# Strassen's scheme for the last group's product with w4 in an attention and S2-MLP kernel

## The chip, the cores and the metric

The kernel runs on one core of one Trainium2 chip. The metric is the device time of one execution in microseconds (us). Each time is a median over runs of the same kernel.

## The reference, cut to what matters

x has 2048 rows of 512 float32 columns. The two layers below are applied twice, with the same weights:

```python
def _A_ref(x, wqkv, wo):            # 32 heads of 16, window of 8 keys at a stride of 2 rows
    qkv = (x @ wqkv).reshape(B, S, 3, H, Dh)...
    logits = einsum("bhsd,bhswd->bhsw", q, kg) * scale   # kg: keys of rows s, s-2, .. s-14
    attn = softmax(where(mask, logits, -1e9))
    o = einsum("bhsw,bhswd->bhsd", attn, vg)
    return o.reshape(B, S, D) @ wo
def _B_ref(x, w1, w2, w3, w4):      # D = 512, F = 1792
    h = gelu(layernorm(x) @ w1)
    hs = concat(h's four quarters, shifted by +1, -1, +2, -2 rows) @ w2
    x1 = x + hs
    return x1 + gelu(layernorm(x1) @ w3) @ w4
x = x + _A_ref(layernorm(x), wqkv, wo)
x = x + _B_ref(layernorm(x), w1, w2, w3, w4)
```

## The kernel before

**Tiles and groups.** The rows are cut into four blocks of 512 rows, each of four tiles of 128. Two layers of four blocks make eight groups, n = 0 to 7. Because of the row shifts, a group's second half is skewed: `group(n)` (line 1298) gives the tiles (n,1), (n,2), (n-1,3), (n,0), and for group 7 also its own last tile (7,3), so that group 7 has five tiles. A group passes through the normalisation and the product with wqkv (`p1_stream`), attention on VectorE (`p2`), the product with wo and w1 (`p3`, line 1180), the product with w2 with a layernorm and a transpose (`p4`), and the MLP with w3, gelu and w4 (`p5`, line 1491).

**Precision.** An operand of a product is kept as two fp16 parts, high and low. Each block product is three matmuls (`HLS`, line 51: high·high, high·low, low·high), accumulated in PSUM. So the three matmuls of 512 columns that belong to one tile and one chunk of w4 are one product with w4.

**The MLP.** F = 1792 is cut into 14 chunks of 128. For groups 0 to 5 each chunk makes a product with w3, a gelu, a cast into two fp16 parts, and a product with w4 that adds into one PSUM accumulator per tile (`acc`). For groups 6 and 7 (`FAST`, line 1307) the product with w3 goes by Strassen's scheme: `p5_pair` (line 1397) takes two chunks at once, and makes seven products of quarter blocks instead of eight. These use sums of blocks of w3, made once by `sums_w3` (line 993) and kept in DRAM (`w3s_d`), and sums of blocks of x (`sums_x`, line 1310). VectorE and POOL combine the seven products into the two chunks; gelu and the casts follow. The fifth tile of group 7 is computed plainly beside them (`up5`). Then come the products with w4 of the pair, in `p5_pair`'s `down`: for each chunk four tiles by three matmuls of 512 columns, which add into `acc`, and the fifth tile's three.

**Order.** No engine's order is that of the source. Each operation gets a key from the table `PLACES` (line 57), by the order in which it is made; `plan` (line 295) sorts all operations by the key, hands out buffer slots in that order, and the instructions are then issued, on each engine in that order (`InOrder`, line 326). A second table, `OTHER`, says for which operations the second of two engines is taken (`op(key, [(POOL, ...), (DVE, ...)])`). An `after=` argument only restricts the table; on the chip an instruction waits for the data that it reads and for the buffer that it writes. DMAs leave SyncE in order, on eight semaphores in turn: each also waits until the one eight places before it on its semaphore has landed. All instructions are recorded at the helper's line 336 (344 after the change), so groups in the profile are told apart by the names of the tiles, not by lines. The names of tiles that matter: `prod`, `kv`, `q`, `L`, `o` belong to attention; `oT`, `nT` are transposed operands; `g` holds the cast gelu outputs; `w` (and `wq_hl`, slots lent from the weights wqkv after their last use) the streamed weights; `mm` and `acc` are PSUM tiles.

Of the kernel before, what the change touches and what calls it, by code (L numbers as in the profile page):

```python
# [1614 lines left out]
```

## Time and profile before

| | us |
|---|---|
| median of 3 runs (1124.87, 1128.14, 1127.88) | 1127.88 |
| the profiled execution, as it was timed | 1126.82 |
| its span in the profile | 1125.0 |
| busy VectorE (DVE), ScalarE (ACT), GpSimd (POOL) | 936.3, 652.0, 498.4 |
| data moved by DMA, mean rate | 224.00 MB, 199 GB/s |

The page gives, for each engine, the busy time over the span. PE is TensorE's matmuls, PEld its weight loads, which overlap the matmuls. SPq and ACTq stand for the DMAs that SyncE and ScalarE issue. A row of a timeline has the start, the length, the engine, the line, the operation, the output tile, the inputs, the shape and a count xN; in brackets stands the idle time of that engine just before, and what ended it. A windows row has the span of time, its length, then the busy time of PE, PEld, DVE, ACT and POOL with their instruction counts, TensorE's granted clock, the share of DMA engines busy and GB/s. The granted clock is 1.00 in every stretch of this profile.

### The profile page before, as it was taken

What the parts mean: (1) busy time and instruction counts of PE and PEld (TensorE: products, weight loads), DVE (VectorE), ACT (ScalarE), POOL (GpSimd) and SP (SyncE); (2) the same over time, 40 slices, a digit from 0 to 9 for tenths busy, and PEclk for the clock granted to TensorE, in tenths of its full rate; (3) what the DMA queues carried; (4) which work ended last, traced back from release to release, by engine and by line L of the source; (5) the groups of instructions that cost most, each with busy time, mean ns of one, the idle gap of its engine ahead of it and who ended that gap; (6) DMA issues with size and microseconds to landing.
All of it is one profiled execution on the core that took longest, in us unless ns stands there. A gap on an engine that the chain in (4) does not pass through costs nothing.

```text
span 1125.0 us, 16122 instructions
## 1 busy us (share of the span) xinstructions
PE 1106.7 (98%) x5488; PEld 550.7 (49%) x5488; DVE 936.3 (83%) x1065; ACT 652.0 (58%) x1233; POOL 498.4 (44%) x587
## 2 busy tenths in 40 slices
PE   9999999999999999999999999999999999999998
PEld 7544444544444444444444444444444447555764
DVE  5899999999999799788988999778996999746432
ACT  5877785358753576365665566573554654467341
POOL 3569674236722473135544143445623367234230
PEclk9999999999999999999999999999999999999999
DMA  7688999999988589766779868996877769555642
GB/s 215 197 226 225 236 245 262 248 237 239 238 233 241 116 209 193 200 161 167 189 182 222 200 156 221 249 240 174 203 223 198 211 160 243 155 145 111 185 146 61
DMA packets 268994, 224.00 MB, mean 199 GB/s; under 512 B 143688, under 2 KB 205128, under 8 KB 268912
## 3 DMA queue, kind: packets, MB, share of 16 engines
q1 hardware_dynamic: 267296, 221.20, 77.1%
q10 hardware_dynamic: 1616, 1.77, 0.6%
q8 instruction: 43, 0.70, 0.3%
q14 instruction: 39, 0.32, 0.1%
HBM read 143.65 MB, written 41.54 MB: 165 GB/s over the span
## 4 chain that ended last, share of the span: by engine, by line
PE 69%; DVE 14%; POOL 5%; ACT 4%; DMA 3%; issue 3%; SPq 1%; ACTq 0%; DVEq 0%; POOLq 0%
PE mm L336 50%; PE acc L336 19%; DVE prod L336 8%; DVE L L336 2%; POOL small L336 2%; DVE f L336 1%; ACT junk L336 1%; SPq L336 1%; POOL f L336 1%; DMA w<-in_B_w_dram 1%; DVE mx L336 1%; POOL prod L336 1%; ACT f L336 1%; DVE g L336 1%; POOL g L336 1%
## 5 line engine op out<-in xcount | busy, mean ns | idle before, releaser
L336 PE MATMUL acc<-w,g 128*128 128x512 f16 (+1 forms) x1104 | 271.2, 395 | 0.4 <-DVE g L336 0.4
L336 PE MATMUL mm<-wq_hl,xt 128*128 128x512 f16 x1008 | 224.9, 379 | 3.0 <-DMA xt<-f 1.6
L336 PE MATMUL mm<-nT,w 128*128 128x512 f16 (+2 forms) x1110 | 225.3, 355 | 1.8 <-DMA nT<-f 1.4
L336 PEld LDWEIGHTS <-w 128*128 128x128 f16 x1428 | 133.9, 98 | 118.1 <-issue 8.4
L336 PEld LDWEIGHTS <-g 128*128 128x128 f16 x1176 | 114.7, 98 | 135.4 <-DVE g L336 1.4
L336 PEld LDWEIGHTS <-xt 128*128 128x128 f16 x1008 | 98.4, 98 | 121.7 <-issue 3.4
L336 DVE TENSOR_TENSOR prod<-kv,L 128x2048 f32<-128x2048 f32 x64 | 150.4, 2350 | 1.4 <-POOL o L336 0.2
L336 DVE TENSOR_REDUCE L<-prod 128x128 f32<-128x2048 f32 x64 | 146.1, 2283 | 1.1
L336 DVE TENSOR_TENSOR prod<-kv,q 128x2048 f32<-128x2048 f32 x58 | 134.3, 2316 | 5.0 <-DMA q<-q_d 1.9
L336 ACT ACTIVATE mm<-mm,s_w 128x512 f32<-128x512 f32 (+1 forms) x109 | 70.1, 644 | 112.1 <-PE mm L336 111.8
L336 DVE TENSOR_TENSOR prod<-prod 128x1024 f32<-128x1024 f32 (+1 forms) x119 | 124.8, 1049 | 2.5
L336 POOL TENSOR_SCALAR small<-small 128x1 f32<-128x1 f32 (+1 forms) x133 | 65.1, 490 | 103.8 <-ACT junk L336 56.2
L336 POOL TENSOR_TENSOR small<-small,nhalf 128x1 f32<-128x1 f32 (+1 forms) x104 | 90.2, 869 | 46.0 <-ACT small L336 40.6
L336 PE MATMUL mm<-w_hl,h 128*128 128x512 f16 x384 | 86.3, 379 | 0.0
L336 PE MATMUL mm<-nT,w_hl 128*128 128x512 f16 x384 | 85.8, 379 | 0.0
L336 PE MATMUL mm<-wo_hl,oT 128*128 128x512 f16 x336 | 74.2, 379 | 0.0
L336 POOL TENSOR_TENSOR g<-f,g 128x512 f16<-128x512 f32 x34 | 42.5, 1252 | 52.8 <-ACT g L336 26.3
L336 PEld LDWEIGHTS <-oT 128*128 128x128 f16 x426 | 41.7, 98 | 49.3 <-issue 0.6
L336 ACT ACTIVATE ev<-mm,s_kv 128x512 f32<-128x512 f32 x56 | 38.0, 682 | 38.5 <-PE mm L336 31.7
L336 PEld LDWEIGHTS <-w_hl 128*128 128x128 f16 x384 | 37.6, 98 | 44.9
L336 PEld LDWEIGHTS <-h 128*128 128x128 f16 x384 | 37.6, 99 | 44.4 <-POOL h L336 0.2
L336 POOL TENSOR_TENSOR o<-prod 128x256 f32<-128x256 f32 x22 | 16.8, 766 | 89.5 <-DVE prod L336 89.2
(251 smaller groups left out, 1611.1 us busy)
## 6 DMA issues: line engine op xcount, KB each, us to landing
w<-w SPq DMA_DIRECT2D x183, 256.0 KB, 3.7
kv<-kv_d SPq DMA_DIRECT2D x112, 352.0 KB, 5.8
w<-in_B_w_dram SPq DMA_DIRECT2D x56, 256.0 KB, 3.8
kv_d<-ev SPq DMA_DIRECT2D x112, 128.0 KB, 3.5
q_d<-ev SPq DMA_DIRECT2D x28, 256.0 KB, 5.5
w<-g SPq DMA_DIRECT2D x28, 256.0 KB, 3.2
q<-q_d SPq DMA_DIRECT2D x28, 256.0 KB, 4.3
wq_hl<-w SPq DMA_DIRECT2D x27, 256.0 KB, 4.2
```

Of the source, the lines that this page charges most:

```text
L336: i = f(*a, **k).ins
```

## The change

In group 7 the product with w4 for the first four tiles is now made by Strassen's scheme too. It is no longer inside the pairs, but follows after all of them, in seven products over the whole of F ("sweeps"):

- `sums_w4(j)`, for each of the seven pairs: loads two chunks of w4 as float32 (256 KB each), makes two blocks of sums in four operations of 256 columns, casts both into high and low parts, and stores them in DRAM (`w4s_d`, two stores of 256 KB).
- In `p5_pair` of group 7, after the gelu: four operations of 256 columns make the sums `s12`, `s34` of the two chunks' outputs; these two tiles are cast into high and low parts as well. All four casts of a pair are kept until the end, in 28 lent slots of kind `gg`: 16 in the tiles of attention (kv, q, prod, L, o) after group 7's last product with wo, and four each in the weights wo, w1 and w2 after their last use. The products of a pair with w4 are left only for the fifth tile (two times three matmuls of 512 columns).
- `p5_sweep`: seven products, each over seven pairs, each with its own half of a weight block per pair (a DMA of 128 KB in pieces of 512 bytes), for two tile positions q: 14 accumulations of 21 matmuls of 256 columns. Results leave PSUM by 256 columns, and are added to the output rows in place by VectorE (`into_x`).
- The tables `PLACES` and `OTHER` are new as a whole.

The diff, cut to its core (the two tables are left out):

```diff
+    small_w = {n: const.tile([P, 2 * NC * D], F16, name=f"{n}_hl") for n in ("wo", "w1", "w2")}
+    late = ([as16("kv", j, k) for j in range(3) for k in range(2)] + [as16("q", j, 0) for j in range(2)] +
+            [as16("prod", 0, k) for k in range(4)] + [as16("L", j, 0) for j in range(2)] + [as16("o", j, 0) for j in range(2)] +
+            [of_w(n, k) for n in ("wo", "w1", "w2") for k in range(4)])
+        "gg": places("gg", 0, [P, 2 * D], F16, const, late),
+    def sums_w4(j, after):
+        raw = [Buf("w") for _ in range(2)]
+        for m, t in enumerate(raw):
+            dma(0, lambda t=t: f32v(t.t, D), lambda i=2 * j + m: w4_d[P * i:P * (i + 1), :], [], [t], 1.0, after)
+        def sums(e):
+            e.tensor_sub(t12.t[:, h1], b1[:, h2], b1[:, h1])
+            e.tensor_sub(t12.t[:, h2], b2[:, h2], t12.t[:, h1])
+            e.tensor_sub(t34.t[:, h1], b2[:, h2], b1[:, h2])
+            e.tensor_sub(t34.t[:, h2], b2[:, h1], t12.t[:, h2])
+        op(0, [(POOL, 2.5, lambda: sums(G), None), (DVE, 1.5, lambda: sums(V), "lock")], raw, [t12, t34])
+        for m, t in enumerate((t12, t34)):
+            hi_of(0, D, out, src, w, [t, iv4], [hl])
+            rest(0, lambda out=out: out(1), src, w, lambda out=out: out(0), D, [hl, iv4], [t, (hl, 1)])
+            dma(0, lambda m=m: w4s_d[j][:, m], lambda hl=hl: halves(hl.t), [(hl, [0, 1])], [(w4s, (j, m))], 1.0)
...
+        end_group = K > NT
-        gs = [Buf("g") for _ in cs]
+        gs = [Buf("gg" if end_group else "g") for _ in cs]
...
+            def sums(e):
+                a1, a2 = got[0].t, got[1].t
+                e.tensor_add(s12.t[:, L], a1[:, R], a2[:, R])
+                e.tensor_sub(s12.t[:, R], s12.t[:, L], a1[:, L])
+                e.tensor_sub(s34.t[:, L], a1[:, L], a1[:, R])
+                e.tensor_sub(s34.t[:, R], a2[:, L], s12.t[:, R])
...
-            pe(key, 0.6478 * NT, lambda down=down: down(range(NT)), [w, (gs[q], [0, 1])], acc[:NT])
             if gx:
                 pe(key, 0.6478, lambda down=down: down([NT]), [w, (gx, [0, 1])], acc[NT:])
+            else:
+                pe(key, 0.6478 * NT, lambda down=down: down(range(NT)), [w, (gs[q], [0, 1])], acc[:NT])
+    def p5_sweep(n, key, xt_):
+        def product(k):
+            ws = [Buf("w") for _ in range((NP + 1) // 2)]
+            for j in range(NP):
+                dma(key, lambda j=j: hb(ws[j // 2], j % 2), lambda j=j: src(j), [cell(j)], [(ws[j // 2], j % 2)], 0.5, past[-2])
+            for q, kind in enumerate(("mm", "acc")):
+                def sweep(ps=ps, q=q, k=k):
+                    for j in range(NP):
+                        v = halves(kept[j][gi].t)[:, :, 2 * P * gh + P * q:2 * P * gh + P * (q + 1)]
+                        for a, b in HLS:
+                            T.matmul(ps.t[:, L], v[:, a], hb(ws[j // 2], j % 2)[:, b], start=(m == 0), stop=(m == 3 * NP - 1))
+        def into_x(r, h, q, v, rd):
+            dve(key, 0.42, lambda: V.scalar_tensor_tensor(x.t[:, h], v(), s_w4.t, x.t[:, h], ALU.mult, ALU.add), ...)
+        for q, ps in enumerate(product(1)):
+            act(key, 0.42, lambda ps=ps, q=q: A.activation(half(a, q), ps.t[:, L], AF.Copy), [ps], [(a, q)])
+            into_x(0, L, q, lambda q=q: half(a, q), [(a, q)])
...
+        for k, r, h in ((2, 0, L), (3, 0, R), (4, 1, L)):
+            for q, ps in enumerate(product(k)):
+                into_x(r, h, q, lambda ps=ps: ps.t[:, L], [ps])
...
-        acc = [Buf("acc" if k < NT else "mm") for k in range(K)]
+        acc = [Buf("acc" if k < NT or n >= FAST else "mm") for k in range(K)]
...
+        if n == N - 2:
+            for j in range(NP):
+                sums_w4(j, [w2_last[n - 1]])
```

What the new tables make of the order is shown at three places, in rows of the programs as they are issued. A row has the line, the operation, the output tile, its inputs, the shape, and in brackets the semaphores that it waits for (DMAHW0 to DMAHW7 are the eight of the DMAs).

On SyncE, the last loads of weights before the change. They are whole blocks (128x1024) of w3, w4 and the sums of w3, among output rows:

```order
L336 DMA w_193<-w_9_128 128x1024 [waits DMAHW2_49,PE_49]
...
L336 DMA w_170<-w_8_127 128x1024 [waits DMAHW7_49,PE_49]
L336 DMA wq_hl<-w_10_129 128x1024 [waits DMAHW0_49,PE_49]
L336 DMA w_194<-w_11_130 128x1024 [waits DMAHW1_49,PE_49]
L336 DMA w_167<-w_13_132 128x1024 [waits DMAHW2_49,PE_49]
L336 DMA out_dram<-x_200 64x512 [waits DMAHW3_49]
L336 DMA wq_hl<-w3s_139 128x1024 [waits DMAHW4_49,PE_49]
```

On SyncE, the loads after the change of product 2 of the sweeps: seven halves (128x2x256) of the chunks 1, 3, ... 13 of w4, into four slots. The loads of five products are issued ahead of these, and those of product 4 behind them.

```order
L344 DMA w_175<-w_3_125 128x2x256 [waits DMAHW4_49,PE_49]
L344 DMA w_180<-w_5_127 128x2x256 [waits DMAHW5_49,PE_49]
L344 DMA w_201<-w_11_133 128x2x256 [waits DMAHW6_49,PE_49]
L344 DMA w_180<-w_7_129 128x2x256 [waits DMAHW0_49]
L344 DMA w_201<-w_9_131 128x2x256 [waits DMAHW1_49]
L344 DMA wq_hl<-w_13_135 128x2x256 [waits DMAHW2_49,PE_49]
L344 DMA w_175<-w_1_123 128x2x256 [waits DMAHW3_49]
```

The last loads before the change are spread among other transfers, with a wait of their own for PE each; after it seven halves stand in a train, and the last of the train is the one for the first pair.

On TensorE, the last products before the change are the fifth tile's accumulations, with no wait among them:

```order
L336 MATMUL mm_69<-w_194,oT_219 128x512
L336 LDWEIGHTS oT_224
L336 MATMUL mm_69<-wq_hl,oT_224 128x512
L336 LDWEIGHTS oT_224
...
L336 LDWEIGHTS oT_224
L336 MATMUL mm_69<-w_167,oT_224 128x512
```

On TensorE, after the change, near the end of the program: the last matmuls of a sweep of product 3 (into acc_230) and the first of product 2 (into acc_228; `kv_185` and `kv_214` are lent slots, that hold cast gelu outputs here):

```order
L344 MATMUL acc_230<-w_203,w_hl 128x256 [waits DMAHW7_49]
...
L344 LDWEIGHTS kv_185 [waits DMAHW3_49]
L344 MATMUL acc_228<-w_175,kv_185 128x256 [waits DVE_49]
...
L344 MATMUL acc_228<-w_175,kv_214 128x256 [waits DMAHW4_49]
...
L344 MATMUL acc_228<-w_180,prod_208 128x256 [waits DMAHW5_49]
```

In place of 512 columns under no wait there are 256 columns, and a sweep's first weight load now waits for the DMA on semaphore 3, which is the last row of the train above.

On VectorE, in the middle of group 7's attention before the change (`prod` from `kv` and the weights `L`, folded by halves; `h` and `f` belong to group 6's products with w1 and w2):

```order
L336 TENSOR_TENSOR prod_196<-kv_209,L_197 128x2048 [waits DVE_49]
L336 TENSOR_TENSOR prod_196<-prod_196 128x2x512 [waits DVE_49]
L336 SCALAR_TENSOR_TENSOR h_187<-mm_71,c_h,h_187 128x512 [waits Activation_49]
L336 SCALAR_TENSOR_TENSOR h_187<-mm_69,c_h,h_187 128x512 [waits Activation_49]
L336 SCALAR_TENSOR_TENSOR h_187<-mm_73,c_h,h_187 128x512 [waits Activation_49]
L336 TENSOR_TENSOR prod_196<-prod_196 128x2x256 [waits DVE_49]
```

The same place after the change (`w` slots hold raw chunks of w4; `f` and `prod_213` here take the sums of `sums_w4`):

```order
L344 TENSOR_TENSOR f_183<-w_201,f_217 128x256 [waits DVE_49]
L344 TENSOR_TENSOR prod_208<-kv_214,L_209 128x2048 [waits Pool_49]
L344 TENSOR_TENSOR prod_208<-prod_208 128x2x512 [waits DVE_49]
L344 TENSOR_TENSOR f_215<-w_175 128x256 [waits DMAHW7_49,DMAHW0_49]
L344 TENSOR_TENSOR f_215<-w_188,f_215 128x256 [waits DMAHW6_49,DVE_49]
L344 TENSOR_TENSOR prod_213<-w_188,w_175 128x256
L344 TENSOR_TENSOR prod_213<-w_188,f_215 128x256 [waits DVE_49]
L344 SCALAR_TENSOR_TENSOR h_192<-mm_74,c_h,h_192 128x512 [waits Activation_49]
L344 SCALAR_TENSOR_TENSOR h_192<-mm_70,c_h,h_192 128x512 [waits Activation_49]
```

Four operations of 256 columns of `sums_w4`, two of which wait for loads of raw w4, now stand between a product of attention and the next step of attention.

More of the change, by code (lines that the diff above doesn't have):

```diff
@@ L372, in tile_mixer @@
     NT_OWN, W_OWN = 2, 8
+    small_w = {n: const.tile([P, 2 * NC * D], F16, name=f"{n}_hl") for n in ("wo", "w1", "w2")}
+    as16 = lambda kind, j, k: (lambda: slots[kind][j].bitcast(F16)[:, 2 * D * k:2 * D * (k + 1)])
+    of_w = lambda n, k: (lambda: small_w[n][:, 2 * D * k:2 * D * (k + 1)])
+    late = ([as16("kv", j, k) for j in range(3) for k in range(2)] + [as16("q", j, 0) for j in range(2)] +
+            [as16("prod", 0, k) for k in range(4)] + [as16("L", j, 0) for j in range(2)] + [as16("o", j, 0) for j in range(2)] +
+            [of_w(n, k) for n in ("wo", "w1", "w2") for k in range(4)])
+    LENT_A = [("gg", j) for j in range(16)]
+    LENT_WO, LENT_W1, LENT_W2 = [[("gg", 16 + 4 * m + j) for j in range(4)] for m in range(3)]
     wq_t = const.tile([P, 2 * NC * 3 * D], F16, name="wq_hl")
@@ L456, in tile_mixer @@
     w3s = Buf()
+    w4s_d = [dram.tile([P, 2, 2, 512], F16, name=f"w4s_{c}") for c in range(NP)]
+    w4s = Buf()
     def dma(key, out, in_, r, w, xfer, after=(), by_act=False, late=0.0, d=0.53):
@@ L522, in tile_mixer @@
     wqv = wq.t.rearrange("p (a c f) -> p a c f", a=2, c=NC)
-    wo, w1, w2 = [keep(f"{n}_hl", [P, 2 * NC * D], F16) for n in ("wo", "w1", "w2")]
+    wo, w1, w2 = [Buf(None, small_w[n]) for n in ("wo", "w1", "w2")]
     def rows(ap, b, i, par):
@@ L1017, in sums_w3 @@
             dma(0, lambda m=m: w3s_d[j][:, m], lambda hl=hl: halves(hl.t), [(hl, [0, 1])], [(w3s, (j, m))], 1.0)
+    def sums_w4(j, after):
+        op.stage = ("sums_w4", j)
+        raw = [Buf("w") for _ in range(2)]
+        t12, t34 = [Buf("f32") for _ in range(2)]
+        for m, t in enumerate(raw):
+            dma(0, lambda t=t: f32v(t.t, D), lambda i=2 * j + m: w4_d[P * i:P * (i + 1), :], [], [t], 1.0, after)
+        def sums(e):
+            b1, b2 = [f32v(t.t, D) for t in raw]
+            h1, h2 = slice(0, 2 * P), slice(2 * P, D)
+            e.tensor_sub(t12.t[:, h1], b1[:, h2], b1[:, h1])
[3 more added lines that the diff above has]
+        op(0, [(POOL, 2.5, lambda: sums(G), None), (DVE, 1.5, lambda: sums(V), "lock")], raw, [t12, t34])
+        at0 = NF + 2 * j
+        iv4, w = iv[len(FOURS) + j // 2], inv_p.t[:, at0:at0 + 1]
+        for m, t in enumerate((t12, t34)):
+            hl = Buf("g")
+            out = lambda a, hl=hl: halves(hl.t)[:, a]
+            src = lambda t=t: t.t
+            hi_of(0, D, out, src, w, [t, iv4], [hl])
+            rest(0, lambda out=out: out(1), src, w, lambda out=out: out(0), D, [hl, iv4], [t, (hl, 1)])
+            dma(0, lambda m=m: w4s_d[j][:, m], lambda hl=hl: halves(hl.t), [(hl, [0, 1])], [(w4s, (j, m))], 1.0)
     iv_of = iv[:len(FOURS)]
@@ L1174, in tile_mixer @@
     hs, n1_st, w2_last = {}, {}, {}
+    wo_ops, w1_ops, w2_ops = [], [], []
     def hview(h):
@@ L1211, in p3 @@
             if not early:
-                pe(key + 0.01 * i, 2.591, fn, [*[(t, both) for t in oTs[n]], x, (wo, whole)], [ps],
-                   after=[w2_last[n - 1]])
+                wo_ops.append(pe(key + 0.01 * i, 2.591, fn, [*[(t, both) for t in oTs[n]], x, (wo, whole)], [ps],
+                                 after=[w2_last[n - 1]] + (wo_ops[-3:] if n == N - 1 and i == NT - 1 else [])))
+                if n == N - 1 and i == NT - 1:
+                    wo_ops[-1].lend = LENT_A + LENT_WO
             src = lambda x=x: x.t
@@ L1250, in fn @@
                         m += 1
-            pe(key + 0.1, 2.591, fn, [(nT, [(i, a) for i in range(NT) for a in range(2)]), (w1, whole)],
-               [ps, (h, "new")])
+            w1_ops.append(pe(key + 0.1, 2.591, fn, [(nT, [(i, a) for i in range(NT) for a in range(2)]), (w1, whole)],
+                             [ps, (h, "new")], w1_ops[-3:] if n == N - 1 and g == NC - 1 else ()))
+            if n == N - 1 and g == NC - 1:
+                w1_ops[-1].lend = LENT_W1
             hi, lo = [lambda a=a, g=g: hb()[:, a, g, OWN[g]:OWN[g] + D] for a in range(2)]
@@ L1352, in fn @@
                         j += 1
-            w2_last[n] = pe(key + 0.01 * k, 2.591, fn, [(h, h_cells(i)), (w2, whole)], [ps])
+            w2_last[n] = pe(key + 0.01 * k, 2.591, fn, [(h, h_cells(i)), (w2, whole)], [ps],
+                            w2_ops[-4:] if n == N - 1 and k == NT else ())
+            w2_ops.append(w2_last[n])
+            if n == N - 1 and k == NT:
+                w2_last[n].lend = LENT_W2
             dve(key, 0.75, lambda ps=ps, x1=x1, s=s: V.scalar_tensor_tensor(
@@ L1413, in p5_pair @@
         xa, xs_ = x2T[n][0], xT2[n]
-        gs = [Buf("g") for _ in cs]
-        gx = Buf("oT") if K > NT else None
+        end_group = K > NT
+        gs = [Buf("gg" if end_group else "g") for _ in cs]
+        gx = Buf("oT") if end_group else None
         def prod(ps, h, w, wh, x, xh, xt):
@@ L1470, in out @@
             if pool:
-                rest(key, lambda: gv(1), src, cg, lambda: gv(0), wd, [c_g, (g, 0)], [(buf, cells), (g, 1)])
+                rests.append(lambda: rest(key, lambda: gv(1), src, cg, lambda: gv(0), wd, [c_g, (g, 0)], [(buf, cells), (g, 1)]))
             else:
@@ L1474, in out @@
                     gv(1), src(), cg, gv(0), ALU.mult, ALU.subtract), [(buf, cells), c_g, (g, 0)], [(g, 1)])
+        rests = []
         for q, c in enumerate(cs):
             out(c, lambda q=q: got[q].t, got[q], [0, 1], gs[q], D, True)
+            if not end_group:
+                rests.pop()()
         if gx:
             out(cs[0], lambda: end.t[:, L], end, [0], gx, 2 * P, False)
+        if end_group:
+            s12, s34 = [Buf("f32") for _ in range(2)]
+            def sums(e):
[4 more added lines that the diff above has]
+                e.tensor_sub(s34.t[:, R], a2[:, L], s12.t[:, R])
+            op.stage = ("s5", n)
+            op(key, [(POOL, 2.5, lambda: sums(G), None), (DVE, 1.5, lambda: sums(V), "lock")], [(t, [0, 1]) for t in got], [s12, s34])
+            op.stage = ("p5", n)
+            for f in rests:
+                f()
+            op.stage = ("s5", n)
+            for t in (s12, s34):
+                g = Buf("gg")
+                gs.append(g)
+                gv = lambda a, g=g: halves(g.t)[:, a]
+                cg = c_g.t[:, cs[0]:cs[0] + 1]
+                hi_of(key, D, gv, lambda t=t: t.t, cg, [t, c_g], [(g, 0)])
+                rest(key, lambda gv=gv: gv(1), lambda t=t: t.t, cg, lambda gv=gv: gv(0), D, [c_g, (g, 0)], [t, (g, 1)])
+            op.stage = ("p5", n)
+            kept.append(gs)
         for q, (c, w) in enumerate(zip(cs, w4)):
@@ L1557, in p5 @@
                 pe(key, 0.6478 * (k1 - k0), down, [w4, (g, [0, 1])], acc[k0:k1])
+        if n == N - 1:
+            p5_sweep(n, base, [xs[(*lb[m], i)] for m, i in tiles[:NT]])
         for k, (m, i) in enumerate(tiles):
@@ L1560, in p5 @@
             x = xs[l, b, i]
+            if n == N - 1 and k < NT:
+                for p in range(2):
+                    dma(base, lambda b=b, i=i, p=p: rows(out_d, b, i, p),
+                        lambda x=x, p=p: par_of(x.t, p), [x], [], 0.5, by_act=p == 1)
+                continue
             more = {} if l else {"accum_out": x_sum[b].t[:, i:i + 1]}
```

38 lines of the change are left out of this document (added), and 356 rows, old and new, of tables (OTHER, PLACES).

## The prediction

> **What bounds the kernel now.** I read the page first, then windows over stretches of the span, then the timelines of the end and of group 7's attention.
>
> ```profile
> PE 1106.7 (98%) x5488; PEld 550.7 (49%) x5488; DVE 936.3 (83%) x1065; ACT 652.0 (58%) x1233; POOL 498.4 (44%) x587
> PE 69%; DVE 14%; POOL 5%; ACT 4%; DMA 3%; issue 3%; SPq 1%; ACTq 0%; DVEq 0%; POOLq 0%
> ```
>
> TensorE (PE) is busy for 1106.7 of 1125.0 us, so waits hold at most 18.3 us in all. Time can leave only with PE's work, with those waits or with the tail. The chain of waits has DVE in it with 14%: VectorE is the engine that comes next.
>
> ```profile
> core 0: us, PE busy (x) PEld busy (x) DVE busy (x) ACT busy (x) POOL busy (x), PEclk, DMA share, GB/s
> 100.00:200.00 100.00, 94.77 (x445) 45.01 (x444) 96.53 (x112) 67.10 (x129) 68.53 (x72) 1.00 0.96 247
> ...
> 900.00:950.00 50.00, 48.85 (x300) 29.23 (x299) 48.74 (x55) 28.80 (x52) 35.04 (x31) 1.00 0.74 185
> ...
> 1020.00:1100.00 80.00, 80.00 (x618) 54.20 (x617) 31.97 (x61) 35.73 (x65) 25.92 (x30) 1.00 0.57 160
> 1100.00:1110.00 10.00, 10.00 (x74) 5.94 (x72) 4.22 (x9) 2.37 (x4) 0.00 (x0) 1.00 0.01 2
> 1110.00:1125.00 15.00, 10.49 (x49) 4.58 (x47) 3.60 (x6) 1.44 (x2) 1.85 (x2) 1.00 0.33 87
> ```
>
> Where the products of group 7 with w3 and w4 run (1020 to 1110) PE never waits, and DVE, ACT and POOL are under half busy. In 1110 to 1125 PE is busy for 10.49: the other 4.5 us are the tail behind the last matmul. At 900 to 950, in group 7's attention, DVE is 97% busy. So the change must gain in PE's work at the end, and can lose either there or where it hands DVE more to do.
>
> **PE's work: −4.2.** The timeline of PE at the end gives both forms:
>
> ```profile
> 1096.30 2.75 PE L336 MATMUL acc<-w,g 128*128 128x512 f16 x12
> 1098.89 1.47 PE L336 MATMUL mm<-nT,w 128*128 128x256 f16 x12
> 1100.20 2.75 PE L336 MATMUL acc<-w,g 128*128 128x512 f16 x12
> ...
> 1106.69 1.50 PE L336 MATMUL mm<-xt,w 128*128 128x128 f16 x24
> 1108.03 2.75 PE L336 MATMUL acc<-w,g 128*128 128x512 f16 x12
> ```
>
> Twelve of 512 columns take 2.59 from start to next start (1098.89 − 1096.30), 0.216 each; twelve of 256 take 1.31, 0.109 each; 24 of 128 take 1.34. Removed are 14 chunks x 12 = 168 of 512, which is 14 x 2.59 = 36.3. Added are 14 sweeps x 21 = 294 of 256: 21 x 0.109 = 2.29 a sweep, 32.1 in all. The difference is −4.2: seven products in place of eight, with no loss for the shorter form. The Trainium skill speaks against this: "TensorE: Matmul & The Clock Gate", section "Back-to-back issue gap", gives sustained streams about 131 ns for 512 columns but 81 ns for 128; a line through these gives an estimate of 98 ns for 256, by which 168 would cost 22.0 and 294 28.8, and the change would lose 6.8 here. The rows above (216 and 109 ns) disagree with it.
>
> **The tail: −0.4.**
>
> ```profile
> 1120.53 0.75 DVE L336 SCALAR_TENSOR_TENSOR x<-mm,s_w,x 128x512 f32<-128x512 f32 x1 [1.17 <-PE mm L336]
> 1120.82 1.27 ACTq L336 DMA_DIRECT2D out_dram<-x  x2
> ```
>
> Behind the last matmul stand one evacuation of 512 columns (0.75) and a pair of output DMAs. The evacuation is 256 columns wide afterwards; a DVE operation of 256 takes 0.42 (rows below). That is −0.33, and I take −0.4, as fewer rows are left to go out at the end. Bounds: 0 and −1.
>
> **The sweeps' loads: +2.2.** Before the change a block of weights is a load of 256 KB used for 2.59 us of PE; after it a half block of 128 KB is used for 2 x 3 matmuls, 0.65 us. The sweeps run, by the changed order, as products 1, 6, 1, 6, 5, 7, 5, 7, 3, 2, 3, 2, 4, 4. Each product needs four of twelve slots, so products 5 and 7 load when 1 (after the third sweep) and 6 (after the fourth) are done or from slots left by the pairs, 3 and 2 when 6 and 5 are done, 4 when 7 is done. Product 5's second sweep is the seventh, product 2's first is the tenth: product 2's train leaves only when the seventh ends, and has the eighth and ninth sweeps, 4.58 us, to land.
>
> ```profile
> 1080.04 1.75 SPq L336 DMA_DIRECT2D out_dram<-x  x3
> ```
> ```profile
> DMA to landing us min/median/max: 2.6/3.2/3.8
> ```
> ```profile
> kv_d<-ev SPq DMA_DIRECT2D x112, 128.0 KB, 3.5
> ...
> wq_hl<-w SPq DMA_DIRECT2D x27, 256.0 KB, 4.2
> ```
>
> The first row is a train on SyncE's queue: three in 1.75, 0.58 each, and I take 0.6. The second is the answer on tile w in 1060 to 1080, with a little traffic beside it: a load of 256 KB lands 2.6 to 3.8 after its issue. The third is of the page: 128 KB in short pieces takes 3.5. Lone halves of 128 KB in pieces of 512 bytes are not in this trace; I bound them by 2.6 and 4.2 and take 2.8, near the quiet loads. The load that product 2's sweep needs first is the last of its seven: 0.1 + 6 x 0.6 + 2.8 = 6.5, so PE waits for 1.9 (bounds 1.7 and 3.3). The same sum for product 7, whose first load leaves fourth, gives 0.3; for 3 and 4, whose first pairs are issued early, nothing, with a slack of 1 to 2 us. Sum +2.2, bounds 1.5 and 5 if several trains meet the long end. By the Trainium skill, "DMA: Bandwidth & Descriptors", section "Anatomy of one DMA" (about 2.0 us fixed and bytes over 436 GB/s, fitted to another issue path), 128 KB is estimated at 2.3, and the wait at 1.4 in place of 1.9; the trace's shortest landing for that tile, 2.6 for twice the bytes, agrees with it, though no row here shows the form.
>
> **sums_w4: +0.7.** The nearest rows are the same steps for w3 on DVE, and two on POOL:
>
> ```profile
> 758.67 0.42 DVE L336 TENSOR_TENSOR f<-w 128x256 f32<-128x256 f32 x1
> ...
> 759.80 0.42 DVE L336 TENSOR_TENSOR f<-w,f 128x256 f32<-128x256 f32 x1
> ...
> 769.41 0.88 DVE L336 SCALAR_TENSOR_TENSOR g<-f,inv_p,g 128x512 f16<-128x512 f32 x1
> ```
> ```profile
> L336 POOL TENSOR_TENSOR g<-f,g 128x512 f16<-128x512 f32 x34 | 42.5, 1252 | 52.8 <-ACT g L336 26.3
> ...
> L336 POOL TENSOR_TENSOR o<-prod 128x256 f32<-128x256 f32 x22 | 16.8, 766 | 89.5 <-DVE prod L336 89.2
> ```
> ```profile
> 953.02 2.77 POOL L336 TENSOR_TENSOR ev<-f,ev 128x256 f32<-128x256 f32 x1
> ```
>
> A block of sums is four operations, 1.5 on DVE (758.67 to 760.13 where the next one starts); a low half is 0.88 there, 1.25 and a multiplication on POOL. The tables leave 15 of these steps to DVE and 8 to POOL; between the first product of group 7's attention and its last cast DVE gets about 9 us more. The rows at both ends of that stretch:
>
> ```profile
> 849.22 2.29 DVE L336 TENSOR_TENSOR prod<-kv,q 128x2048 f32<-128x2048 f32 x1 [1.72 <-DMA kv<-kv_d]
> 855.78 0.75 DVE L336 SCALAR_TENSOR_TENSOR prod<-mm,s_wo,prod 128x512 f32<-128x512 f32 x1 [4.27 <-PE mm L336]
> ...
> 971.94 0.75 DVE L336 SCALAR_TENSOR_TENSOR f<-o,c_o,f 128x512 f16<-128x512 f32 x1
> ```
> ```profile
> 972.72 1.23 SPq L336 DMA_TRANSPOSE oT<-f  x1
> ```
> ```profile
> 971.99 1.47 PE L336 MATMUL mm<-wq_hl 128*128 128x256 f16 x12 [0.87 <-DVE f L336]
> ...
> 976.46 10.52 PE L336 MATMUL mm<-wo_hl,oT 128*128 128x512 f16 x48
> ```
>
> DVE idles for 4.27 at 851.5 to 855.8, which takes in about half of the 9. The rest delays the last cast (971.94) by 3 to 5 us. From its end at 972.7 to the product with wo at 976.46 lie 3.8 us, in which the transpose lands: PE came without a wait, so up to 2 us of that are slack, and by the changed order PE has 1.3 us more to do ahead of it. So 0 to 2 us are left as a wait of PE; I take 0.7 (bounds −1, as the new order may take out the 0.87 before 971.99, and 3). The 2.77 us row shows POOL's operation of 256 columns beside DVE at 3.6 times the usual 0.77, so the long end can't be excluded.
>
> **p4 to p5 in group 7: +0.5.** The fifth tile's accumulator moves from `mm` to `acc`, and its product with w2 comes last of five now.
>
> ```profile
> 1010.22 13.11 PE L336 MATMUL mm<-w_hl,h 128*128 128x512 f16 x60
> 1023.17 5.34 PE L336 MATMUL acc<-wq_hl,g 128*128 128x512 f16 x24
> ```
>
> Before, PE covers the layernorm behind these 60 matmuls with group 6's last products (5.34 and on). The changed order keeps such a cover of about 10 us, over a chain that took about as long: 0 to 1.5, taken as 0.5.
>
> **The pairs of group 7: +0.9.** Without four tiles' products with w4 a pair holds 42 matmuls of 256 (4.59) and the fifth tile's 1.34 + 6 x 0.216 = 1.30: 7.2 us of PE. The rows of the timeline of DVE and of the groups in 1042 to 1100 that price the other engines:
>
> ```profile
> 993.60 0.69 DVE L336 TENSOR_TENSOR f<-mm,ev 128x512 f32<-128x512 f32 x1 [1.35 <-PE mm L336]
> 994.33 0.42 DVE L336 TENSOR_TENSOR prod<-mm,f 128x256 f32<-128x256 f32 x1
> ```
> ```profile
> L336 DVE SCALAR_TENSOR_TENSOR oT<-mm,c_g,oT 128x256 f16<-128x256 f32 x3 | 1.4, 483 | 4.6 <-ACT oT L336 4.6
> ```
> ```profile
> L336 ACT ACTIVATE f<-f,s_w 128x512 f32<-128x512 f32 x9 | 6.5, 717 | 17.6 <-DVE f L336 17.6
> L336 ACT ACTIVATE g<-f,c_g 128x512 f16<-128x512 f32 x9 | 6.4, 719 | 1.0 <-PE acc L336 0.8
> ```
>
> Beside it DVE has per pair the additions from PSUM (0.69 + 4 x 0.42), the fifth tile's half (0.5), and now most sums and a part of the low halves, 14 us more over 7 pairs, so 2.0 a pair: up to 6.3 in all. ACT has two gelus and three to four casts of 0.72 and about 1.5 of copies and the fifth tile, 5.7; POOL two to three low halves, 4 to 5. All are below 7.2, but DVE's margin is small, where it was over half idle. No product of the next pair waits for a cast; it waits for PSUM to be emptied by DVE and ACT. Bounds 0 and 3 (0.4 a pair), and I take 0.9, near the short end.
>
> **Elsewhere: 0 ± 1.5.** The whole order is new, and about 13 us of PE's waits lie before 1020 (18.3 less the tail's 4.5), 5.2 of them in 100 to 200; they can shift either way.
>
> **The sum**: −4.2 − 0.4 + 2.2 + 0.7 + 0.5 + 0.9 = −0.3. The profiled execution took 1126.82 (span 1125.0 and 1.8 around it), 1.1 below the median of the runs shown. So I predict **1126.5**: PE's saving is real, and is given back as waits.
>
> **The rivals.**
> (a) The waits are hidden: products 2 and 7 find their loads at 2.6 with little wait (1.2), DVE's extra work in attention stays within its idle time and the pairs run without a stall. Then −4.2 − 0.4 + 1.2 = −3.4, and with an earlier order that takes out 1 us of the start's waits 1122.4. For it: PE did not wait once in 1020 to 1110. Against: the train of seven behind a single release.
> (b) Slower: DVE becomes the bound in group 7's attention. There it is 97% busy, gets 9 us more and has POOL beside it slowed by it; if less than 4 us of this fit in, the last transpose lands over 2 us after PE has run out of other work, and each further us is a us of the end. With the full 9 less the slack of 3.3 it costs 5.7 in place of 0.7: 1131.5. It decides from a delay of the last cast of 3.3 us.
> (c) The sweeps are bound by loads: at a landing of 4.2 and a train of seven for each of products 5, 7, 2 and 3, waits come to 4 to 6: 1129.
> (d) The change doesn't do what it says: the rows of the new order show the sweeps, so this holds no chance.
>
> **How the numbers follow.** Forecast (the sum within 2 us) 0.45; (a) 0.28; (b) 0.15; (c) 0.12. The skill's rule on issue gaps gets none beyond these, as the rows contradict it. Two in ten outside leaves 1121 to 1132; the forecast's own range is 1124.5 to 1128.5. A measurement of this kernel can tell 0.3%, 3.4 us, from no change: faster is below 1124.5, slower above 1131.3. Faster takes nearly all of (a) and a little of the forecast, 0.31; slower half of (b), a third of (c) and the long ends of several terms at once, 0.20; the same 0.49.
>
> **What would show it.** After: 14 runs of 21 matmuls of 256 columns at 2.29 each, and PE's busy time 4 us lower. One wait of 1.4 to 3.3 of PE for a load ahead of product 2's first sweep and one below 1 ahead of 7's; the last operation on DVE 0.42; the first product of group 7 with wo 0 to 2 us after its wait for oT begins; DVE near 85% busy in the pairs. I am wrong if PE's wait for oT passes 3, if matmuls of the sweeps start over 0.12 apart, or if the time of the early groups moves by over 2 us.

## The result and the profile after

The change made the kernel slower. The median is 1146.41 us (1141.69 to 1148.76, 4 runs) against 1126.38 us for the kernel before (1124.26 to 1128.14, 4 runs): a ratio of 1.017, with a 95% interval of 1.0148 to 1.0193, so 17 to 22 us. The profiled execution has a span of 1144.7 us.

The page of the changed kernel, in the same parts as before (span; busy time of each engine; the granted clock of TensorE in 40 slices):

```profile
span 1144.7 us, 16716 instructions
PE 1109.2 (97%) x5614; PEld 564.1 (49%) x5614; DVE 987.7 (86%) x1132; ACT 668.3 (58%) x1265; POOL 566.0 (49%) x628
PEclk9999999999999999999999999999999989999999
```

PE's busy time did not fall by 4.2 us, as the work did: it rose by 2.5. And PE is idle for 35.5 us of the span in place of 18.3. DVE has 51 us more, POOL 68. The summary of PE's waits (waiting tile, what it waited for, us in total, times, longest) has a few new entries at its head:

```profile
PE acc L344 <- ACT g L344: 5.9, 2, 5.0
PE mm L344 <- DVE f L344: 5.3, 6, 2.0
PE mm L344 <- DMA xt<-f: 4.2, 4, 1.5
PE mm L344 <- DMA nT<-f: 3.0, 2, 2.7
PE acc L344 <- POOL g L344: 1.6, 1, 1.6
```

The timeline of PE has where they stand, from 800 us to the sweeps. Counted by its matmuls, PE's products of group 5's MLP run until 944 there, with group 6's product with wo in between (859.77); so the first three rows are group 5's, and 935.65 is the last but one of its 14 chunks. Group 6's own products with w4 begin at 965.43. Group 7's attention is on VectorE from 857 on:

```profile
830.10 2.33 PE L344 MATMUL acc<-w,g 128*128 128x512 f16 x10 [1.18 <-DVE g L344]
857.18 2.75 PE L344 MATMUL mm<-nT,w 128*128 128x512 f16 x12 [1.45 <-ACT g L344]
...
935.65 1.04 PE L344 MATMUL acc<-wq_hl,g 128*128 128x512 f16 x2 [5.03 <-ACT g L344]
...
954.25 4.09 PE L344 MATMUL mm<-wq_hl,w 128*128 128x256 f16 x36 [1.97 <-DVE f L344]
...
971.54 2.33 PE L344 MATMUL acc<-w,g 128*128 128x512 f16 x10 [1.62 <-POOL g L344]
...
995.15 3.19 PE L344 MATMUL mm<-wo_hl,oT 128*128 128x512 f16 x14
...
1066.70 0.83 PE L344 MATMUL mm<-nT,wq_hl 128*128 128x256 f16 x6 [1.60 <-DMA wq_hl<-w]
...
1085.11 1.47 PE L344 MATMUL mm<-nT,w 128*128 128x256 f16 x12 [1.15 <-DVE oT L344]
1088.90 1.47 PE L344 MATMUL mm<-nT,w 128*128 128x256 f16 x12 [0.98 <-DVE f L344]
...
1107.54 0.82 PE L344 MATMUL acc<-wq_hl,kv 128*128 128x256 f16 x6
...
1109.84 0.49 PE L344 MATMUL acc<-wq_hl,kv 128*128 128x256 f16 x3
...
1128.75 0.83 PE L344 MATMUL acc<-w,kv 128*128 128x256 f16 x6 [0.41 <-DMA w<-w]
```

The longest wait, 5.03 us, is for a cast of group 5's gelu outputs. The timeline of ScalarE shows it behind group 6's layernorm (`f<-prod,small`) in the same queue; `mm<-mm,s_w` is the last gelu of group 5, and casts of its last two chunks (`f<-mm,c_g`, `g<-mm,c_g`) follow:

```profile
923.90 0.81 ACT L344 ACTIVATE f<-prod,small 128x512 f32<-128x512 f32 x1 [3.03 <-POOL small L344]
...
931.55 0.64 ACT L344 ACTIVATE mm<-mm,s_w 128x512 f32<-128x512 f32 x1
933.75 0.69 ACT L344 ACTIVATE f<-mm,c_g 128x512 f32<-128x512 f32 x1 [1.56 <-issue]
934.34 1.26 ACT L344 ACTIVATE g<-mm,c_g 128x512 f16<-128x512 f32 x2
```

The product of group 7 with wo (995.15) begins without a wait, but 18.7 us later than before (976.46). The sweeps begin at 1107.54, and take 2.30 us each (to 1109.84). The windows behind two of the waits, and in the pairs (columns as before):

```profile
185.00:200.00 15.00, 15.00 (x66) 7.87 (x65) 14.62 (x13) 4.80 (x7) 3.12 (x2) 0.91 1.02 278
925.00:936.00 11.00, 5.97 (x28) 2.48 (x26) 10.36 (x9) 7.71 (x16) 9.90 (x12) 0.96 0.76 203
936.00:945.00 9.00, 8.57 (x31) 3.44 (x30) 7.90 (x9) 3.30 (x6) 5.93 (x5) 0.67 0.59 140
1056.00:1097.00 41.00, 36.33 (x361) 31.04 (x361) 33.26 (x60) 21.67 (x38) 18.94 (x20) 1.00 0.76 227
```

Behind the wait of 5.03 us the granted clock is 0.67 for 9 us: 3 us of PE's time lost on top of the wait. Behind a wait of 2.7 for `nT`, at 184, it is 0.91 for 15 us, 1.4 more. These 4.4 us are most of why PE's busy time rose while its work fell. The second of them is chance of this trace: e1 and e4 below have the same wait (2.67 and 2.68 us), with a clock of 1.00 behind it. In the pairs of group 7 PE idles for 4.7 of 41 us, with DVE at 81%; 1.6 of the 4.7 is a wait for a load of weights (1066.70), and nearly all the rest is for VectorE; before the change DVE had 40% in such a stretch.

The starts of matmuls on PE's timeline say where time went, in this kernel and in the ones tried below (us from the start of the span; "lag" is against the kernel before; the last column is from the last matmul with w2 of group 7 to the last matmul of all):

| run | wo, group 6 | wo, group 7 | lag | last matmul | w2 of group 7 to the end |
|---|---|---|---|---|---|
| before | 852.99 | 976.46 | | 1120.12 | 97.16 |
| after | 859.77 | 995.15 | 18.7 | 1140.12 | 99.75 |
| e1, no sums_w4 | 855.56 | 983.53 | 7.1 | 1127.99 | 99.28 |
| e2, no gelu sums | 860.66 | 995.44 | 19.0 | 1136.27 | 95.64 |
| e3, neither | 857.43 | 985.41 | 9.0 | 1126.22 | 95.62 |
| e4, order alone | 855.03 | 982.86 | 6.4 | 1125.21 | 97.16 |

Single traces differ by up to 2.8 us as early as group 1's product with w2 (239.71 in e4, 242.53 in e2), ahead of all that these runs leave out, so a lag holds to some 2 us.

So nearly all was lost ahead of group 7's product with wo, where the change only prepares (1.3 of the 18.7 us is PE's own work, 12 matmuls of 256 columns that now stand ahead of this product); the part that holds the sweeps is 2.6 us longer than before, with 4.1 us less work in it.

### The profile page after: what moved, and what is told of

It reads as the page before. It is cut to its first block, busy times and chain, and to the rows that moved or that the text cites. A ratio compares the mean times of both kernels' runs of the same rounds, so it can differ in the third digit from the quotient of the medians.

```text
span 1144.7 us, 16716 instructions
## 1 busy us (share of the span) xinstructions
PE 1109.2 (97%) x5614; PEld 564.1 (49%) x5614; DVE 987.7 (86%) x1132; ACT 668.3 (58%) x1265; POOL 566.0 (49%) x628
## 4 chain that ended last, share of the span: by engine, by line
PE 48%; DVE 12%; DMA 5%; issue 5%; POOL 4%; ACT 3%; SPq 1%; POOLq 0%; DVEq 0%; ACTq 0%
PE mm L344 34%; PE acc L344 14%; DVE prod L344 5%; DVE f L344 4%; POOL small L344 1%; POOL f L344 1%; DMA kv<-kv_d 1%; DVE g L344 1%; ACT f L344 1%; SPq L344 1%; DMA wq_hl<-w 1%; DVE L L344 1%; DMA kv_d<-ev 1%; DMA w<-in_B_w_dram 1%; DVE x L344 1%
## 5 line engine op out<-in xcount | busy, mean ns | idle before, releaser
L344 PE MATMUL mm<-nT,w 128*128 128x512 f16 (+2 forms) x1158 | 234.5, 356 | 7.9 <-DMA nT<-f 2.7
L344 PE MATMUL acc<-w,g 128*128 128x512 f16 (+1 forms) x924 | 229.8, 399 | 3.6 <-POOL g L344 1.6
L344 PEld LDWEIGHTS <-w 128*128 128x128 f16 x1464 | 139.2, 98 | 128.8 <-issue 17.1
L344 PEld LDWEIGHTS <-g 128*128 128x128 f16 x1008 | 98.8, 98 | 129.0 <-ACT g L344 5.5
L344 DVE TENSOR_TENSOR prod<-kv,L 128x2048 f32<-128x2048 f32 x64 | 152.0, 2374 | 4.5 <-POOL o L344 3.4
L344 DVE TENSOR_REDUCE L<-prod 128x128 f32<-128x2048 f32 x64 | 146.1, 2283 | 1.2
L344 DVE TENSOR_TENSOR prod<-prod 128x512 f32<-128x512 f32 (+2 forms) x115 | 120.6, 1049 | 2.8
L344 POOL TENSOR_TENSOR small<-small,nhalf 128x1 f32<-128x1 f32 (+1 forms) x104 | 86.7, 836 | 55.9 <-ACT small L344 52.4
L344 POOL TENSOR_SCALAR small<-small 128x1 f32<-128x1 f32 (+1 forms) x130 | 77.9, 601 | 73.0 <-ACT junk L344 45.1
L344 POOL TENSOR_TENSOR g<-f,g 128x512 f16<-128x512 f32 x32 | 46.4, 1455 | 58.2 <-ACT g L344 27.5
L344 POOL TENSOR_TENSOR o<-prod 128x256 f32<-128x256 f32 x29 | 26.2, 902 | 88.7 <-DVE prod L344 73.8
L344 PEld LDWEIGHTS <-w_hl 128*128 128x128 f16 x474 | 46.3, 98 | 46.8 <-issue 1.2
```

The costliest lines, as they stand in the source:

```text
L344: i = f(*a, **k).ins
```

## The experiments

**Leaving out sums_w4 (e1, e1b).**

```diff
     for o in plan(op.ops, slots):
+        if o.stage[0] == "sums_w4":
+            continue
         o.fn()
-        from_s = lambda m, h: (lambda j: w4s_d[j][:, m][:, :, h], ...
+        from_s = lambda m, h: (lambda j: w34_d[2 * j + m][:, 1][:, :, h], ...
```

> Leaves out all of sums_w4 (its loads, sums, casts and stores); the sweeps read plain blocks of w4 from DRAM in place of the sums, by DMAs of the same form. Same order for all the rest. The changed kernel takes 1146.4 us. Theory A (the steps of sums_w4 stand on VectorE, ScalarE and POOL in front of the layernorm chain of group 6 and in group 7's attention, and TensorE waits): 11 to 15 us below the changed kernel, 1131 to 1135, the 5 us wait near 930 and the half clock after it gone. Theory B (the new order is worse by itself, whatever is in it): within 3 us of the changed kernel. Theory C (the traffic of sums_w4, 7 MB more, delays other transfers): as A, but then the run that keeps the DMAs stays slow.

In the second run only the arithmetic goes, and the loads and stores stay:

```diff
+        if o.stage[0] == "sums_w4" and "dma" not in o.alts[0][2].__qualname__:
+            continue
-            dma(0, lambda m=m: w4s_d[j][:, m], lambda hl=hl: halves(hl.t), ...
+            dma(0, lambda m=m: w4s_d[j][:, m], lambda: halves(small_w["w1"][:, :2 * D]), ...
```

> Leaves out the arithmetic of sums_w4, and keeps its 14 loads and 14 stores (the stores write fp16 parts of w1, so the sweeps multiply by other numbers). Theory A: within 2 us of the run without any of sums_w4. Theory C: within 3 us of the changed kernel, 1143 to 1149.

Measured: 1134.34 us (ratio to before 1.0065, 1.0045 to 1.0086) and 1133.95 us (1.0055, 1.0035 to 1.0076). So sums_w4 costs 12 us, and all of it is its arithmetic: the 28 DMAs cost nothing that can be measured. Theory A holds for its size, theory C falls, and theory B as the whole cause. The wait of 5.03 shrinks to 1.47, and the clock is 1.00 behind it:

```profile
927.12 0.61 PE L345 MATMUL acc<-wq_hl,g 128*128 128x512 f16 x2 [1.47 <-ACT g L345]
```

In the traces three places make some 10 of the 12 us: 3.6 by this wait, 3.4 by the clock (0.51 from 935 to 942 in the changed kernel), and 3.1 by waits of PE from 800 us to here (830.10 and 857.18 among them), of which e1 has none. ScalarE's last gelu of group 5 starts 11.5 us after the last part of group 6's product with w2 in e1 (924.02 and 912.54) and 14.1 us after it in the changed kernel (931.55 and 917.50).

**Leaving out the sums of the gelu outputs (e2), and both (e3).** In e3 the stages are `("sums_w4", "s5")`, and the loads those of e1.

```diff
     for o in plan(op.ops, slots):
+        if o.stage[0] == "s5":
+            continue
         o.fn()
...
-                        v = halves(kept[j][gi].t)[:, :, ...]
+                        v = halves(kept[j][gi if gi < 2 else 0].t)[:, :, ...]
```

> Leaves out the sums s12 and s34 of the gelu outputs of group 7 and their casts; the sweeps of the products that use them read the first chunk's cast tile instead. Theory D (the waits of TensorE in the pairs, 5.6 us in 1056 to 1096, come of VectorE, ScalarE and POOL having more to do per pair than the pair's 7.2 us of TensorE cover): 5 to 7 us below the changed kernel, 1139 to 1141. Theory E (the pairs wait because their own products with w4 no longer stand between as cover): within 2 us of the changed kernel.

> Leaves out both: sums_w4 whole, and the sums of the gelu outputs with their casts. What is left of the change are the sweeps and the new order. Theories A and D together: the sum of both gains, 1124 to 1129, so the level of the kernel before. Theory B: still over 1138.

Measured: 1142.43 us (1.0132, 1.01 to 1.0163) and 1131.26 us (1.004, 1.0025 to 1.0054). The gelu sums cost 3 to 4 us, a little below what theory D gave and above theory E's 2. For sums_w4, e3 against e2 gives 11 us, close to the 12 of e1. The table has the same by place: from w2 to the end 95.64 in place of 99.75, and DVE's load in the pairs falls from 33.26 to 23.58:

```profile
1056.00:1097.00 41.00, 40.02 (x391) 33.74 (x389) 23.58 (x47) 22.45 (x38) 9.02 (x10) 1.00 0.80 245
```

Without both, the part with the sweeps is 1.5 us shorter than before the change; that is what is left there of the 4.1 us of work. But the kernel is still 5 us above the one before, outside what theories A and D (1124 to 1129) and theory B (over 1138) gave, and 9.0 us late at the product with wo, where only the order of the change is left.

**The order alone (e4).** The kernel before, with `PLACES` and `OTHER` such that all up to group 7's first product with w2 stands in the changed kernel's relative order:

```diff
-PLACES = [...]   # of before
+PLACES = [...]   # the order of after up to group 7's first product with w2, then that of before
```

> The work of the kernel before (plain products with w4, no sums_w4), with its operations in the changed kernel's relative order, and its choice of engines, up to the first product of group 7 with w2; from there on the old order. Nothing is left out. Theory B' (the order that was made for the added steps is itself worse for TensorE, as what is left at run e3 says: 5 us above the kernel before with 4 us less of TensorE work): 5 to 9 us above the kernel before, 1131 to 1135. Theory A alone (only the added steps cost): within 2 us of the kernel before.

Measured: 1132.13 us (1.0057, 1.0042 to 1.0073), 6 us above the kernel before, with the same work. Theory B' holds, beside theory A. The choice of engines goes with the order here (VectorE has 1045 instructions in place of 1065, POOL 600 in place of 587); e4 does not tell the two apart. The timeline of PE has the price in a few places:

```profile
698.70 2.75 PE L341 MATMUL mm<-nT,w 128*128 128x512 f16 x12 [1.11 <-DVE g L341]
...
926.06 0.60 PE L341 MATMUL acc<-w,g 128*128 128x512 f16 x2 [0.94 <-ACT g L341]
927.53 2.33 PE L341 MATMUL acc<-w,g 128*128 128x512 f16 x10 [0.86 <-DVE g L341]
...
941.96 2.78 PE L341 MATMUL mm<-wq_hl,w 128*128 128x256 f16 x24 [0.84 <-DVE f L341]
...
959.26 2.33 PE L341 MATMUL acc<-wq_hl,g 128*128 128x512 f16 x10 [1.62 <-POOL g L341]
```

In the kernel before, PE does not wait at the first three; it waits for 1.15 where it waits for 0.84 here, and for 0.20 where it waits for 1.62. These are the places of the changed kernel's waits as well: group 4's product with w3 (698.70), group 5's last products with w4 (926.06, 927.53) and group 6's first ones with w3 and w4. I read this as an order that has PE ask for these casts so early that each further step on VectorE, POOL or ScalarE makes them late; no run tests that by itself.

**Which engine's steps (e5).** The steps of one engine in sums_w4 become fills with zeros (shown for POOL), or are dropped:

```diff
+        def short(e):
+            e.memset(t12.t, 0.0)
+            e.memset(t34.t, 0.0)
-        op(0, [(POOL, 2.5, lambda: sums(G), None), (DVE, 1.5, lambda: sums(V), "lock")], raw, [t12, t34])
+        op(0, [(POOL, 2.5, lambda: short(G), None), (DVE, 1.5, lambda: sums(V), "lock")], raw, [t12, t34])
-            rest(0, lambda out=out: out(1), src, w, lambda out=out: out(0), D, ...)
+            op(0, [(DVE, 0.75, lo_dve, "lock"), (POOL, 1.95, lambda out=out: G.memset(out(1), 0.0), None)], ...)
...
+        if o.stage[0] == "sums_w4" and o.alts[OTHER.get(o.seq, 0)][0] == ACT:   # e5_act_out alone
+            continue
```

> The changed kernel, in its order, but what POOL does in sums_w4 (8 steps) is left out: each is one or two fills with zeros at the same place. sums_w4 as a whole costs 12 us. Theory G (POOL's steps do it: they stand among the small steps of group 6's layernorm on POOL, and slow VectorE's operations beside them): 6 to 10 us below the changed kernel, 1137 to 1141. Theory H (VectorE's 15 steps do it): 0 to 4 us below.

> The changed kernel, in its order, but what VectorE does in sums_w4 (15 steps) is left out: each is one or two fills with zeros at the same place. Theory G: 1 to 4 us below the changed kernel. Theory H: 6 to 10 us below, 1137 to 1141. If both are near 6 the two engines share it.

> The changed kernel, in its order, but ScalarE's 12 casts of sums_w4 are left out (the low parts are made from what the buffers held before). VectorE's steps cost 8.5 us of 12 when they alone are cut short, and POOL's 8.8. Theory I (any engine's steps cost, since a layernorm or gelu passes through all three in turn, and each step in a queue delays the chain): 3 to 8 us below the changed kernel, 1138 to 1143. Theory J (only VectorE and POOL are short of time there, ScalarE is busy for 58% of the span and takes its casts in waits): within 2 us of the changed kernel.

Measured: with POOL's steps cut 1137.62 us (1.0101, 1.0083 to 1.0119); with VectorE's 1137.96 (1.0098, 1.0082 to 1.0114); without ScalarE's casts 1143.97 (1.0149, 1.0126 to 1.0173). Against the changed kernel's 1.017 that is 8, 8 and 2 us, and all three together cost 12. Neither G nor H is right alone: POOL's and VectorE's steps cost as much as each other, and their costs don't add up, since they delay the same chain: PE's wait of 5.03 is 3.61 with POOL's steps cut, 2.88 with VectorE's, and 4.80 without ScalarE's casts. For ScalarE's the interval meets that of the changed kernel, so I and J stay open. The timelines of POOL and VectorE in the changed kernel have a meeting of both (sums_w4's steps are the ones with `w`):

```profile
922.03 1.83 POOL L344 TENSOR_SCALAR small<-small 128x1 f32<-128x1 f32 x1
...
930.66 0.72 POOL L344 TENSOR_TENSOR prod<-w 128x256 f32<-128x256 f32 x1
931.46 1.05 POOL L344 TENSOR_TENSOR prod<-w,prod 128x256 f32<-128x256 f32 x1
933.14 1.10 POOL L344 TENSOR_TENSOR f<-w,w 128x256 f32<-128x256 f32 x1 [0.63 <-DVE f L344]
934.21 2.77 POOL L344 TENSOR_TENSOR f<-w,prod 128x256 f32<-128x256 f32 x1
```
```profile
933.59 2.81 DVE L344 TENSOR_TENSOR prod<-kv,q 128x2048 f32<-128x2048 f32 x1
```

The same operation of POOL takes 0.72 and 2.77. The one of 2.77 runs beside an attention product that takes 2.81 on VectorE, where the one at 921.41 takes 2.28. In the pages' groups the small steps of the layernorm on POOL, one column wide, went from 490 ns before to 601 after; but in e4, without sums_w4, they are at 589 already (and at 595 in e1), so this comes with the order and its choice of engines:

```profile
L336 POOL TENSOR_SCALAR small<-small 128x1 f32<-128x1 f32 (+1 forms) x133 | 65.1, 490 | 103.8 <-ACT junk L336 56.2
...
L341 POOL TENSOR_SCALAR small<-small 128x1 f32<-128x1 f32 (+1 forms) x129 | 75.7, 589 | 68.0 <-ACT junk L341 38.9
...
L344 POOL TENSOR_SCALAR small<-small 128x1 f32<-128x1 f32 (+1 forms) x130 | 77.9, 601 | 73.0 <-ACT junk L344 45.1
```

**Another place for the same steps (e6, n1, n2, m2).** If only their place cost, they should be cheap elsewhere. e6 is the kernel before with sums_w4 added, unused, between its other operations at 380 to 660 us:

```diff
+        if n == N - 2:
+            for j in range(NP):
+                sums_w4(j, [])
         p4(n)
         p5(n)
-PLACES = [...]
+PLACES = [...]   # the old order, with the 63 new operations in between
```

> The kernel before, in its own order with its plain products with w4, and sums_w4 added whole but not used: its steps are put in between at 380 to 660 us, and no other operation changes its place (5 of 3807 by one). Theory A (where the steps stand is what costs): 2 to 6 us above the kernel before, under half of the 12 that they cost in the changed kernel. Rival F (VectorE, POOL and ScalarE can't take them anywhere): 10 us or more above.

Measured: 1141.61 us (1.0137, 1.0109 to 1.0166), 15 us above the kernel before. Theory A fails in this form, and rival F's figure (10 or more) holds: at these places, in an order that had hardly a wait there, the steps cost no less than in the changed kernel. The largest single wait, on the timelines of PE and of VectorE:

```profile
650.51 2.75 PE L345 MATMUL mm<-nT,w 128*128 128x512 f16 x12 [3.49 <-DVE h L345]
```
```profile
639.34 0.75 DVE L345 SCALAR_TENSOR_TENSOR g<-f,inv_p,g 128x512 f16<-128x512 f32 x1 [2.06 <-ACT g L345]
...
641.55 3.13 DVE L345 TENSOR_TENSOR prod<-kv,L 128x2048 f32<-128x2048 f32 x1
...
649.71 0.75 DVE L345 SCALAR_TENSOR_TENSOR h<-mm,c_h,h 128x512 f16<-128x512 f32 x1
```

A low half (`g<-f,inv_p,g`) stands on VectorE for 2.06 us, because the high half that it needs comes from ScalarE; all behind it in the queue waits too, an attention product takes 3.13 in place of 2.29, and the cast of `h`, which PE needs, comes late. So here a step costs what it takes and what it waits for, on an engine that works in order and that PE waits for next.

n1 and n2 have an order of their own from some 290 us on (not from group 6 on, as I had expected of n1), made to fill each engine as tightly as the rows' durations let it, with and without sums_w4; m2 keeps the old order to 940 us and has such a one behind that, with all of the change's work.

```diff
-            for j in range(NP):
-                sums_w4(j, [w2_last[n - 1]])
+            for j in range(NP):
+                sums_w4(j, [])
-PLACES = [...]
+PLACES = [...]   # n1, m2; n2 is n1 with the edit of e1
```

> All the work of the changed kernel, in another order: up to group 6 the order of the kernel before, the steps of sums_w4 placed one pair at a time between 370 and 780 us, mostly on POOL and ScalarE, where TensorE never waits and VectorE is less busy; the end of the program ordered anew. Theory A and B' (place, not amount, of the added steps is what costs, and the rest is the order): TensorE's 4 us come through, 1119 to 1124. Rival F (VectorE, ScalarE and POOL can't take the added work anywhere without delaying TensorE, as each has over half of the span busy): over 1130.

> As the run with the sums spread, but with all of sums_w4 left out (the sweeps read plain blocks of w4 by DMAs of the same form). Theory A: within 2 us of that run, so that sums_w4 costs next to nothing there, and 12 us in the changed kernel. Rival F: 6 us or more below it.

> All the work of the changed kernel: the old order up to some 940 us with the steps of sums_w4 where the run e6 has them, and an order of its own from there on. The candidate for a kernel that beats both. From e6's 2 to 6, the 4 us of TensorE's work and 1 to 4 of waits in the pairs: 1124 to 1132; the added work can't be hidden if it is over 1135, and the change can be made to pay if it is under 1122.

Measured: 1199.69 us (1.0651, 1.0616 to 1.0686), 1179.33 us (1.0475, 1.0433 to 1.0517) and 1158.54 us (1.0285, 1.0269 to 1.0301). n1 and m2 miss what I expected by far. In n1 and n2 the order, not the work, is at fault for most of it: n2, which has no sums_w4, is 53 us above the kernel before. They test theory A badly, since everything moved at once; only their difference, 20 us for sums_w4 in an order without slack, says something on the question, and it is in rival F's range (6 or more). m2 repeats e6: from group 1's product with w2 to group 6's with wo PE takes 612.3 us before, 625.9 in e6 and 627.5 in m2, so the same steps in the same places cost 14 and 15 us there. The rest of m2's 32 us lies outside that stretch, and no run takes it apart. No version beat the kernel before.

## Why the prediction was wrong

**What was right.** PE's work: 14 sweeps at 2.30 us, where I had 2.29, and 256 columns cost half of 512. The tail: from the last matmul to the end of the span 4.6 us in place of 4.9, −0.3 for −0.4. p4 to p5 in group 7: a wait of PE of 0.28 (for `nT`, at 1056.29), for +0.5.

**The sweeps' loads, +2.2: mis-sized, 0.4 measured.** The wait is where I put it, ahead of product 2's first sweep (1128.75), but I let the train start when product 5's second sweep (1121.30 to 1123.59) had ended. The timeline of SyncE shows it earlier:

```profile
1122.15 2.70 SPq L344 DMA_DIRECT2D w<-w  x5
```

A slot is free once the sweep has passed the two pairs in it, so the train runs beside the sweep and not behind it; its pitch was 0.54. (For product 7 the prediction's own terms give 0.1 + 3 x 0.6 + 2.8 − 4.58 = 0.1, not its 0.3; PE did not wait there.)

**sums_w4, +0.7: the step that failed; 11 to 12 us measured (e1, e1b, e3 against e2).** I charged it at one place alone, the transpose that group 7's product with wo needs, and had slack there; PE did not wait at that place. What I left out is that the same VectorE, POOL and ScalarE queues also carry group 6's layernorm and, behind it, the last gelus and casts of group 5's MLP, for which PE waited, with 5.03 us at 935.65 and a clock of 0.67 behind. The sign of being wrong that I had named for the early groups came true with it: group 6's product with wo starts 6.8 us later than before (859.77 against 852.99; 855.56 in e1). VectorE's idle 4.27 us that I let half of the work fall into is a wait for PE's own product, not room that holds for the rest of the stretch. I had the operation of 2.77 us on POOL in the trace before as a warning, and let it stand for the long end alone. The runs e5 show that cutting short either engine's steps alone wins 8.

**The order, "elsewhere 0 ± 1.5": failed too; 6 us measured (e4).** I took a new order as neutral, as its early waits could shift either way. It was made with the added steps in it, and even without them PE waits where group 5's MLP ends and group 6's begins.

**The pairs, +0.9: right mechanism in the main, too small.** The table gives 99.75 − 97.16 = 2.6 from w2 on; with −4.1 of work and +0.4 of loads that leaves 6.3 for the pairs. Of it the gelu sums make 4 (e2: VectorE's load in the pairs falls from 81% to 58%), and some 2 remain without them (95.62 − 97.16 + 4.1 − 0.4 = 2.2 in e3). I had named DVE's margin of 6.3 in 7.2 us per pair, and then costed it near the short end. (The terms listed there add up to 4.9; the window of the pairs has 33.26 us of DVE in the time of 5.0 pairs of PE's work, so 6.6 a pair.) A load of weights in the pairs, for which PE waited 1.6, I had no term for; neither e1 nor e2 has a wait for a load above 0.7 there.

The sum: −4.1 − 0.3 + 0.4 + 6.3 + 12 + 6 = 20.3, and 20.0 was measured between the medians; each of the larger terms holds to 1 or 2 us, so that they meet this well is partly luck. Rival (b) had the sign and the engines, but its wait, for the last transpose of group 7's attention, did not occur, and it had 5.7 us for 12; no rival had the order.

What stays open: whether sums_w4 has a cheap place at all. Three placements cost 12, 15 and 20 us. Three places do not show that there is none, and one in VectorE's idle gaps alone was not tried. Even at no cost, e3's tail leaves 1.5 us of the change, and the gelu sums take more than that back.

## What to carry to other kernels

A saving on the engine that bounds must be set against what prepares it on the engines that feed it: here, with TensorE 97% busy, 35 small steps on three in-order engines cost 12, 15 and 20 us of the end at three places. An idle gap of such an engine can be its wait for the bounding engine, as VectorE's 4.27 us were, and is then no room for the steps elsewhere in its queue; ask of each added step what is behind it in its queue, and not only of the one chain that comes to mind. A table of places that is made anew is a change of its own and can be timed alone, with the old work in the new order.
